# Where the short tail of a weight matrix sits, and q as columns in place of rows, in a one-token attention and GLU kernel

## The chip, the cores and the metric

The kernel runs on one core of a Trainium2 chip. The metric is the device time of one execution in microseconds. The kernel before takes 208.78 us, the median of three runs (208.6 to 209.2).

## What is computed

One token `x` of 640 numbers passes a block of attention and then a gated feed-forward block; all inputs are bfloat16.

```
h   = x + Attention(layernorm(x), k_cache, v_cache, wq, wo)
out = h + ( gelu(g) * u ) @ w_down,   g = n @ w_gate,  u = n @ w_up,  n = layernorm(h)
q = layernorm(x) @ wq           640 -> 32 heads of 128
per head: softmax(q . K / sqrt(128)) . V     K, V: 4096 x 128 per head, 32 heads
w_gate, w_up: 640 x 1728        w_down: 1728 x 640
```

K and V are 67 MB of the 84 MB that are read; the weights are the rest. Each weight is used once, so the arithmetic is matrix times vector throughout.

## The kernel before

All loads are issued by SyncE (SP) in one hand-written order: K of the first pair of heads, x, five chunks of wq, and then K and V by pairs of heads (16 pairs, 2 MB each for K and V, three buffers of each), with wo in four parts between them, then w_gate in one piece, w_up in three, and w_down in four (`wd0` to `wd3`). A load into a buffer that is used again waits for the last reader of that buffer (`load_k`, `load_v`); the loads of the feed-forward weights wait for the q stage, whose wq buffer they overwrite (L517).

**Start.** TensorE (PE) turns x into columns, takes the moments, transposes the first pair's K (`pe_transposes`), and then makes q (L318 to L343). In the kernel before q comes as rows: the normalised x (`xn_bf`) is the stationary operand, one column of it at a time, in four column groups of the array (`tile_position`), and 512 columns of wq are the moving operand. Two banks hold the rows (`qr_ps`, cleared by two matmuls with zeros, L319). VectorE and ScalarE copy the two banks to `q_row` (L585, L541), PE transposes them (L341), and VectorE picks the used columns into `q_sb` (L589). Scores of the first pair follow (`pe_scores`).

**Pairs.** A loop of five turns by three pairs: transposes of K, copies of them to SBUF by VectorE and ScalarE, P times V for the pair before, scores, softmax. All are in lock step by semaphores; wo is applied by groups of eight heads.

**End.** After the last pair: sums of the softmax (`totals`, L396), the last P times V, the projection with wo (L404), the moments of h, and then the feed-forward block. `up` (L412 to L425) makes g and then u as columns: for each of five chunks `j` of the 640 inputs, 14 matmuls of one moving column, each with 128 columns of the weight as the stationary operand. Columns 0 to 12 of the result take every 13th column of the weight (`columns(c)`, L408), so that row p of w_down's first 1664 rows falls on partition p // 13 with contiguous memory. The last column stands for the 64 columns that are left over; before, it takes the last 128 columns of the weight, 64 of which are also in the other 13 columns:

```
return slice(c, FULL * P, FULL) if c < FULL else slice(DF - P, DF)
```

The down projection (L431 to L445) goes in the order 13, 0, 1, ..., 12: five matmuls of one moving column for each. For column 13 the last 64 rows of w_down stand on partitions 64 to 127 (`wd0`, L522), and GpSimd (POOL) has cleared partitions 0 to 63 (L471), so that the columns that are taken twice count once. The other 1664 rows come in pieces of 7, 4 and 2 rows per partition (`wd1`, `wd2`, `wd3`, L524). PE waits for each piece (`landed`, L437's five-matmul groups follow).

VectorE computes `hid` from g and u (L651 to L662), adds y to h (L664), PE turns the result into rows (L447), VectorE copies it (L666), and SP writes it out.

Of the kernel before, what the change touches and what calls it, by code (L numbers as in the profile page):

```python
# [10 lines left out]
def kernel(  # L11
# [14 lines left out]
    bf16 = mybir.dt.bfloat16  # L26
# [5 lines left out]
    PE, DVE, ACT, SP, POOL = nc.tensor, nc.vector, nc.scalar, nc.sync, nc.gpsimd  # L32

    P = 128
    D = 640
    DC = D // P
    NH = 32
    DH = 128
# [11 lines left out]
    ON_ACT = (2, 5)  # L50
    DF = 1728
    NFC = 14
    FULL = NFC - 1
    LAST = DF - FULL * P
# [7 lines left out]
    pool = ctx.enter_context(tc.tile_pool(name="all", bufs=1))  # L62
    psum = ctx.enter_context(tc.tile_pool(name="ps", bufs=1, space=bass.MemoryType.PSUM))

    def sb(name, shape, dtype=f32):
        return pool.tile(shape, dtype, name=name, tag=name)
# [8 lines left out]
    wq_sb = big[:, 0 : DC * NH * DH].rearrange("p (c n) -> p c n", c=DC)  # L75
    wg_sb = big[:, 0:W_MLP].rearrange("p (c f) -> p c f", c=DC)
    wu_sb = big[:, W_MLP : 2 * W_MLP].rearrange("p (c f) -> p c f", c=DC)
    wd_sb = big[:, 2 * W_MLP :].rearrange("p (c d) -> p c d", c=NFC)

    ident = sb("ident", [P, P], bf16)  # L80
# [1 line left out]
    mean_f = sb("mean_f", [P, P])  # L82
    row_of = sb("row_of", [P, P // HG], bf16)
    col_of = sb("col_of", [P, HG], bf16)
    zero_b = sb("zero_b", [P, 4 * DH], bf16)
    x_row = sb("x_row", [DC, P], bf16)
    xs = sb("xs", [P, 2 * DC])
    xm = sb("xm", [P, 2])
    xr = sb("xr", [P, 1])
    xn_bf = sb("xn_bf", [P, DC], bf16)  # L90
    q_row = sb("q_row", [P, 2, 4 * DH], bf16)
    q_sb = sb("q_sb", [P, NH], bf16)
    q3 = sb("q3", [P, 2 * UN], bf16)
    e_t = [sb(f"ex{i}", [P, NB, 2], bf16) for i in range(UN)]
# [18 lines left out]
    hid = sb("hid", [P, NFC], bf16)  # L113
# [8 lines left out]
    tp_b = [t.bitcast(bf16) for t in tp]  # L122
    s_bank, o_bank, m_bank, a_bank = bank("s"), bank("o"), bank("m"), bank("a")
    s_ps = s_bank[:, 0 : 2 * NB].rearrange("p (j i) -> p j i", i=2)
    attn_ps = a_bank[:, 0:DC]
    qr_ps = (s_bank, o_bank)
    q_ps = tp_b[0]
    xT = m_bank.bitcast(bf16)[:, 0:DC]
    m_ps = m_bank[:, 16 : 16 + 2 * DC]
    t_ps = m_bank[:, 32 : 32 + HG]  # L130
# [1 line left out]
    g_ps, u_ps, y_ps = tp[0][:, 0:NFC], tp[1][:, 0:NFC], tp[2][:, 0:DC]  # L132
# [14 lines left out]
    S = {n: nc.alloc_semaphore(f"s_{n}") for n in names}  # L147
    done = {"pe": 0, "dve": 0, "act": 0, "pool": 0}
# [15 lines left out]
    def landed(name):  # L164

        PE.wait_ge(S[name], 16)
        PE.sem_inc(S[name], -16)  # L167
# [3 lines left out]
    def wait_pe(value):  # L171
        DVE.wait_ge(S["pe"], value)

    def dve(make, raw=True):

        if raw:
            wait(DVE, "dve", done["dve"])
        return tick("dve", make())
# [19 lines left out]
    def rstd_of(m, r):  # L198
# [6 lines left out]
        for _ in range(2):  # L205
# [3 lines left out]
            dve(lambda: DVE.tensor_tensor(y, y, w[:], ALU.mult))  # L209
        return dve(lambda: DVE.tensor_copy(r[:], y))  # L210

    PE_XT, PE_MOM, PE_QR, PE_Q = 1, 2, 12, 13
    wait_pe(PE_XT)
    dve(lambda: DVE.tensor_copy(xs[:, 0:DC], xT), False)
    DVE_XS = squares(xs)
# [3 lines left out]
    DVE_XN = dve(  # L219
        lambda: DVE.tensor_scalar(  # L220
            xn_bf[:], xs[:, 0:DC], xm[:, 0:1], xr[:], op0=ALU.subtract, op1=ALU.mult
        )
    )
    DVE_Q = DVE_XN + 2

# [20 lines left out]
    def pe_scores(q2, mark):  # L248
        for j in range(NB):
            g, b = divmod(j, GRP)  # L250
            inst = PE.matmul(
                s_ps[:, j, :],
                lhsT=ksb[g][:, b * DH : (b + 1) * DH],
                rhs=q2,
                start=True,
                stop=True,
            )
        mark("s", inst)
# [34 lines left out]
    T = {}  # L293

    def mark_at(key):
        def mark(name, inst):
            T[key, name] = tick("pe", inst)
        return mark
# [4 lines left out]
    N_DVE_T = NG - len(ON_ACT)  # L303
# [3 lines left out]
    start = mark_at("start")  # L307
# [2 lines left out]
    start("xT", PE.transpose(xT, x_row[0:DC, :], ident[0:DC, 0:DC]))  # L310
    PE.wait_ge(S["dve"], DVE_XS)
    pe_moments(xs, start)
    start("zero", PE.matmul(attn_ps, lhsT=zero_b[:, 0:P], rhs=zero_b[:, 0:DC], start=True, stop=False, skip_group_check=True))
    landed("k0")
    pe_transposes(0, 0, 0, mark_at(0))
    PE.wait_ge(S["dve"], DVE_XN)

    for b in range(2):  # L318
        PE.matmul(qr_ps[b][:], lhsT=zero_b[:, 0:P], rhs=zero_b[:], start=True, stop=False, skip_group_check=True)  # L319
    for c in range(DC):  # L320
        landed(f"wq{c}")
        for b in range(2):
            for r in range(4):
                h = 16 * b + 4 * r
                inst = PE.matmul(
                    qr_ps[b][32 * r : 32 * r + 1, :],
                    lhsT=xn_bf[:, c : c + 1],
                    rhs=wq_sb[:, c, h * DH : (h + 4) * DH],
                    start=False,
                    stop=(c == DC - 1),  # L330
                    skip_group_check=True,
                    tile_position=(0, 32 * r),
                )
    start("q rows", inst)
    PE.wait_ge(S["dve_pe"], N_DVE_T)
    PE.wait_ge(S["act_pe"], len(ON_ACT) + 1)
    PE.wait_ge(S["dve"], DVE_Q - 1)
    for b in range(2):
        for i in range(4):
            k = (4 * b + i) * P  # L340
            inst = PE.transpose(q_ps[:, k : k + P], q_row[:, b, i * DH : (i + 1) * DH], ident[:])  # L341
    start("q", inst)
    PE.wait_ge(S["dve"], DVE_Q)  # L343
    pe_scores(q_sb[:, 0:2], mark_at(0))
    PE.sem_inc(S["dve_pe"], -N_DVE_T)
    PE.sem_inc(S["act_pe"], -len(ON_ACT) - 1)
    PE.wait_ge(S["pool"], 8)

    base = done["pe"]
# [36 lines left out]


    n_turned = NP // PG - 1
    D0 = DVE_Q + 2 * n_turned
    D_SPREAD, D_ROW, D_H, D_HC, D_HID, D_Y = D0 + 4, D0 + 5, D0 + 7, D0 + 9, D0 + 9 + 14 + 10, D0 + 9 + 14 + 11  # L390

    end = mark_at("end")
# [14 lines left out]

    def columns(c):  # L408

        return slice(c, FULL * P, FULL) if c < FULL else slice(DF - P, DF)  # L410

    def up(ps, w, loads):  # L412
        for j in range(DC):
            if j in loads:
                landed(loads[j])
            for c in range(NFC):
                inst = PE.matmul(
                    ps[:, c : c + 1],
                    lhsT=w[:, j, columns(c)],
                    rhs=hc[:, j : j + 1],  # L420
                    start=(j == 0 and c == 0),
                    stop=(j == DC - 1),
                    skip_group_check=True,
                )
        return inst  # L425
# [2 lines left out]
    end("g", up(g_ps, wg_sb, {0: "wg"}))  # L428
    end("u", up(u_ps, wu_sb, {0: "wu0", 3: "wu1", 4: "wu2"}))
    PE.wait_ge(S["dve"], D_HID)  # L430
    down = {FULL: "wd0", 0: "wd1", 7: "wd2", 11: "wd3"}  # L431
    order = [FULL] + list(range(FULL))
    for i, c in enumerate(order):
        if c in down:
            landed(down[c])
        for m in range(DC):
            inst = PE.matmul(  # L437
                y_ps[:, m : m + 1],
                lhsT=wd_sb[:, c, m * P : (m + 1) * P],
                rhs=hid[:, c : c + 1],  # L440
                start=(i == 0 and m == 0),
                stop=(i == NFC - 1),
                skip_group_check=True,
            )
# [22 lines left out]

    for _ in range(2):
        spare(POOL).then_inc(S["wo"], 1)
    POOL.wait_ge(S["pe"], T["start", "q"])  # L470
    POOL.memset(wd_sb[0 : P - LAST, FULL, :], 0.0).then_inc(S["pool"], 1)  # L471
    POOL_COPIED = 9
    for g in range(NP // PG - 1):
        POOL.wait_ge(S["wo_in"], 16)
        POOL.sem_inc(S["wo_in"], -16)  # L475
# [7 lines left out]
    def load(name, dst, src):  # L483
        SP.dma_start(dst, src).then_inc(S[name], 16)
# [34 lines left out]
    wu_rows = B_w_up.rearrange("(c p) f -> p c f", p=P)  # L519
    for i, (a, b) in enumerate(((0, 3), (3, 4), (4, 5))):  # L520
        load(f"wu{i}", wu_sb[:, a:b, :], wu_rows[:, a:b, :])
    load("wd0", wd_sb[P - LAST :, FULL, :], B_w_down[FULL * P : DF, :])  # L522
    wd_rows = B_w_down[0 : FULL * P, :].rearrange("(p c) d -> p c d", c=FULL)
    WD = ((0, 7), (7, 11), (11, 13))  # L524
    for i, (a, b) in enumerate(WD):
        load(f"wd{i + 1}", wd_sb[:, a:b, :], wd_rows[:, a:b, :])

# [8 lines left out]
    for n in range(NP):  # L536
        for g in ON_ACT:
            act_copy(n, g)
        if n == 0:
            ACT.wait_ge(S["pe"], PE_QR)  # L540
            ACT.copy(q_row[:, 1, :], qr_ps[1][:]).then_inc(S["act_pe"], 1)  # L541
        ACT.wait_ge(S["pe"], pe_at(n, "s"))
        for i in range(2):
            r = slice(i * HP, (i + 1) * HP)
            inst = ACT.activation(
                e_t[n % UN][r, :, i],
                s_ps[r, :, i],
                AF.Exp,
                scale=SCALE,
                accum_out=rs_all[r, 2 * n + i : 2 * n + i + 1],  # L550
            )
            inst.then_inc(S["act"] if i == 0 else S["act_pe"], 1)
# [25 lines left out]
    def event(inst=None):  # L578
        if inst is None:
# [1 line left out]
        inst.then_inc(S["dve_pe"], 1)  # L581

    dve_copies(0)
    wait_pe(PE_QR)
    dve(lambda: DVE.tensor_copy(q_row[:, 0, :], qr_ps[0][:]), False)  # L585
    wait_pe(PE_Q)
    rows = q_ps.rearrange("p (b i r c) -> p b i r c", b=2, i=4, r=4)[:, :, :, :, 0]
    assert dve(
        lambda: DVE.tensor_copy(  # L589
            q_sb[:].rearrange("p (b r i) -> p b i r", b=2, r=4), rows  # L590
        ),
        False,
    ) == DVE_Q

    def group_of(turn):

# [2 lines left out]
    for turn in range(TURNS):  # L599
# [11 lines left out]
        if turn == 0:  # L611
            wait(DVE, "dve", DVE_Q)
        event(DVE.tensor_copy(q3[:], q_sb[:, 2 * first : 2 * (first + UN)]))
        for i in range(UN):
            n = first + i
# [12 lines left out]
        else:  # L628
            event()

    assert done["dve"] == D0
    wait_pe(T["end", "totals"])
    dve(lambda: DVE.reciprocal(rinv[:], t_ps), False)
    dve(lambda: DVE.tensor_tensor(o_col[:, 0 : HG - 2], o_raw[:, NH - HG : NH - 2], rinv[:, 0 : HG - 2], op=ALU.mult))
    wait_pe(T["end", "pv"])
# [72 lines left out]
```

## Time and profile before

| | |
|---|---|
| runs | 208.6, 209.2, 208.78 us |
| the profiled execution | 208.6 us, of which the span (first to last instruction) is 206.6 us, so 2.0 us lie around it |
| PE busy | 169.8 us (82%) |
| PE weight loads (PEld) busy | 164.3 us (79%) |
| VectorE, ScalarE, GpSimd busy | 81.0, 48.4, 19.8 us |
| bytes moved by DMA | 84.39 MB, 408 GB/s over the span |
| mean granted TensorE clock | 0.715 |

The span is read in three parts: the start up to the first scores at 24.4 us, the pairs up to some 183 us, and the end. Times in the text are microseconds from the start of the span. The form "128\*128 128x1" of a matmul is rows by columns of the stationary operand, and then the output's partitions by elements. The end of a matmul is modelled in the profile, so that the steps between the starts of matmuls are the better measure of their pace.

### The profile page before, as it was taken

Reading aid. Unit: us, or ns where it says so; the run is one execution under the profiler, and the core shown is the slowest. Engines: PE = TensorE matmul, PEld = TensorE weight load, DVE = VectorE, ACT = ScalarE, POOL = GpSimd, SP = SyncE. Lnnn points to the kernel's source line nnn. Section 1 sums busy time; section 2 is a strip of 40 time slices with the busy share of each in tenths; the row PEclk is TensorE's granted clock in tenths of the full one; section 3 lists DMA queues with packets and bytes.
Section 4 is the critical chain, followed back from the end, with each engine's and each line's share of the span. In section 5 each row is a group of like instructions: output and inputs, shape, how many; then the busy total and the mean of one; then the engine's idle time right before and its main releaser. Section 6 shows DMA issues by size and latency. Waiting matters only on the chain. (4 is left out here: it accounts for less than half of the span.)

```text
span 206.6 us, 7735 instructions
## 1 busy us (share of the span) xinstructions
PE 169.8 (82%) x3596; PEld 164.3 (79%) x3597; DVE 81.0 (39%) x199; ACT 48.4 (23%) x99; POOL 19.8 (10%) x21
## 2 busy tenths in 40 slices
PE   0295697995999999889899489999789799983893
PEld 0281497995999999788899489899789799973892
DVE  2182243432535355244435245252517162514230
ACT  0050131311313323132214113131313131310000
POOL 8200100000000006200003500000800000000000
PEclk9999558585666696759696757575757878755555
DMA  6999999999999999999999999999999999999990
GB/s 206 408 428 436 441 415 431 414 431 422 422 425 431 431 417 442 419 423 431 431 419 428 444 419 438 415 431 429 419 444 419 438 422 428 428 406 413 406 355 30
DMA packets 7791, 84.39 MB, mean 408 GB/s; under 512 B 804, under 2 KB 868, under 8 KB 2404
## 3 DMA queue, kind: packets, MB, share of 16 engines
q1 hardware_dynamic: 7780, 84.24, 97.0%
q8 instruction: 8, 0.13, 0.3%
q14 instruction: 3, 0.02, 0.0%
HBM read 84.23 MB, written 0.00 MB: 408 GB/s over the span
## 5 line engine op out<-in xcount | busy, mean ns | idle before, releaser
L562 DVE COPY ksb_67<-tp_117 128x1024 bf16<-128x1024 bf16 x16 | 11.1, 691 | 36.4 <-PE tp_117 L242 36.4
L477 POOL COPY wo<-wo_in 128x5120 bf16<-128x5120 bf16 x3 | 13.3, 4450 | 110.6 <-POOLq L475 56.0
L532 ACT COPY ksb_69<-tp_119 128x1024 bf16<-128x1024 bf16 x16 | 16.2, 1012 | 32.0 <-PE tp_119 L242 32.0
L532 ACT COPY ksb_72<-tp_118 128x1024 bf16<-128x1024 bf16 x16 | 16.2, 1012 | 18.0 <-PE tp_118 L242 17.9
L562 DVE COPY ksb_70<-tp_120 128x1024 bf16<-128x1024 bf16 x16 | 11.1, 691 | 14.8 <-PE tp_120 L242 14.8
L562 DVE COPY ksb_73<-tp_119 128x1024 bf16<-128x1024 bf16 x16 | 11.1, 692 | 6.1 <-PE tp_119 L242 5.9
L262 PE MATMUL o<-ex_94,vt_66 128*128 128x2 bf16 x320 | 8.9, 164 | 5.1 <-PEq L167 4.1
L262 PEld LDWEIGHTS o<-ex_94,vt_66 128*128 128x128 bf16 x320 | 8.7, 98 | 5.6 <-issue 4.4
L562 DVE COPY ksb_68<-tp_118 128x1024 bf16<-128x1024 bf16 x16 | 11.0, 690 | 2.0 <-PE tp_118 L242 1.9
L242 PE MATMUL tp_117<-ident,kt_63 128*128 128x128 bf16 x80 | 9.1, 283 | 3.3 <-PEq L167 3.2
L562 DVE COPY ksb_71<-tp_117 128x1024 bf16<-128x1024 bf16 x16 | 11.0, 688 | 1.6 <-PE tp_117 L242 1.6
L242 PE MATMUL tp_117<-ident,kt_61 128*128 128x128 bf16 x96 | 10.9, 283 | 0.9 <-PEq L167 0.5
L242 PE MATMUL tp_117<-ident,kt_62 128*128 128x128 bf16 x80 | 9.5, 290 | 2.4 <-PEq L167 2.4
L624 DVE COPY o_raw<-o 128x2 f32<-128x2 f32 x15 | 2.4, 159 | 21.8 <-PE o L262 21.8
L242 PE MATMUL tp_118<-ident,kt_61 128*128 128x128 bf16 x96 | 10.9, 282 | 0.0
L562 DVE COPY ksb_74<-tp_120 128x1024 bf16<-128x1024 bf16 x16 | 10.9, 680 | 0.0
L262 PE MATMUL o<-ex_92,vt_64 128*128 128x2 bf16 x384 | 10.6, 163 | 0.0
L262 PEld LDWEIGHTS o<-ex_92,vt_64 128*128 128x128 bf16 x384 | 10.4, 97 | 0.0
L242 PE MATMUL tp_119<-ident,kt_61 128*128 128x128 bf16 x96 | 10.3, 271 | 0.0
L242 PEld LDWEIGHTS tp_117<-ident,kt_63 128*128 128x128 bf16 x80 | 7.3, 131 | 3.5 <-issue 3.5
L242 PE MATMUL tp_120<-ident,kt_61 128*128 128x128 bf16 x96 | 10.0, 266 | 0.0
L242 PEld LDWEIGHTS tp_117<-ident,kt_61 128*128 128x128 bf16 x96 | 8.7, 131 | 1.3 <-DVE ksb_67 L562 0.7
(161 smaller groups left out, 320.3 us busy)
## 6 DMA issues: line engine op xcount, KB each, us to landing
kt_61<-in_A_k_cache_dram SPq DMA_DIRECT2D x6, 2048.0 KB, 25.3
vt_64<-in_A_v_cache_dram SPq DMA_DIRECT2D x6, 2048.0 KB, 27.2
kt_62<-in_A_k_cache_dram SPq DMA_DIRECT2D x5, 2048.0 KB, 24.4
kt_63<-in_A_k_cache_dram SPq DMA_DIRECT2D x5, 2048.0 KB, 26.1
vt_65<-in_A_v_cache_dram SPq DMA_DIRECT2D x5, 2048.0 KB, 28.4
vt_66<-in_A_v_cache_dram SPq DMA_DIRECT2D x5, 2048.0 KB, 30.3
big<-in_A_wq_dram SPq DMA_DIRECT2D x5, 1024.0 KB, 13.0
wo_in<-in_A_wo_dram SPq DMA_DIRECT2D x4, 1280.0 KB, 26.5
```

The lines of the kernel that those rows point to most:

```text
L242: inst = PE.transpose(tp_b[g % NBANK][:, b * DH : (b + 1) * DH], kt[slot][:, g * GRP + b, :], ident[:])
L262: inst = PE.matmul(o_bank[:, 2 * region : 2 * region + 2], lhsT=vt[slot][:, j, :], rhs=e_t[slot][:, j, :], start=(j == 0), stop=(j == NB - 1),
L477: POOL.tensor_copy(wo_t[:], wo_in[:]).then_inc(S["wo"], 1)
L532: ACT.copy(ksb[g][:], tp_b[g % NBANK][:]).then_inc(S["act_pe"], 1)
L562: DVE.tensor_copy(ksb[g][:], tp_b[g % NBANK][:]).then_inc(S["dve_pe"], 1)
L624: event(DVE.tensor_copy(o_raw[:, 2 * n - 2 : 2 * n], o_bank[:, 2 * i : 2 * i + 2]))
```

## The change

Three things are changed together.

1. q is made as columns: 160 matmuls of one moving column (`xn_bf`), each with 128 contiguous columns of wq as the stationary operand, straight into `s_bank[:, 0:32]`; one VectorE copy brings it to `q_sb`. The zero matmuls, `q_row`, its two copies and the eight transposes go.
2. The last 64 columns of w_gate and w_up are taken as 64 columns, so that the matmul for result column 13 writes 64 partitions; the last 64 rows of w_down stand on partitions 0 to 63, and their five matmuls have 64 rows. The clearing on GpSimd goes; VectorE clears partitions 64 to 127 of column 13 of g and u in PSUM (two memsets, after the wait for `totals`).
3. w_down's other rows come in pieces of 8, 4 and 1 rows per partition.

```diff
-    for b in range(2):
-        PE.matmul(qr_ps[b][:], lhsT=zero_b[:, 0:P], rhs=zero_b[:], start=True, stop=False, skip_group_check=True)
     for c in range(DC):
         landed(f"wq{c}")
-        for b in range(2):
-            for r in range(4):
-                h = 16 * b + 4 * r
-                inst = PE.matmul(
-                    qr_ps[b][32 * r : 32 * r + 1, :],
-                    lhsT=xn_bf[:, c : c + 1],
-                    rhs=wq_sb[:, c, h * DH : (h + 4) * DH],
-                    ...
-                    tile_position=(0, 32 * r),
-                )
-    start("q rows", inst)
-    ...
-            inst = PE.transpose(q_ps[:, k : k + P], q_row[:, b, i * DH : (i + 1) * DH], ident[:])
+        for h in range(NH):
+            inst = PE.matmul(
+                q_ps[:, h : h + 1],
+                lhsT=wq_sb[:, c, h * DH : (h + 1) * DH],
+                rhs=xn_bf[:, c : c + 1],
+                start=(c == 0 and h == 0),
+                ...
     start("q", inst)
...
-        return slice(c, FULL * P, FULL) if c < FULL else slice(DF - P, DF)
+        return slice(c, FULL * P, FULL) if c < FULL else slice(FULL * P, DF)
...
                 inst = PE.matmul(
-                    ps[:, c : c + 1],
+                    ps[0 : P if c < FULL else LAST, c : c + 1],
                     lhsT=w[:, j, columns(c)],
...
-    down = {FULL: "wd0", 0: "wd1", 7: "wd2", 11: "wd3"}
+    down = {FULL: "wd0", 0: "wd1", 8: "wd2", 12: "wd3"}
...
+        r = slice(0, P if c < FULL else LAST)
...
-                lhsT=wd_sb[:, c, m * P : (m + 1) * P],
-                rhs=hid[:, c : c + 1],
+                lhsT=wd_sb[r, c, m * P : (m + 1) * P],
+                rhs=hid[r, c : c + 1],
...
-    POOL.wait_ge(S["pe"], T["start", "q"])
-    POOL.memset(wd_sb[0 : P - LAST, FULL, :], 0.0).then_inc(S["pool"], 1)
...
-    load("wd0", wd_sb[P - LAST :, FULL, :], B_w_down[FULL * P : DF, :])
+    load("wd0", wd_sb[0:LAST, FULL, :], B_w_down[FULL * P : DF, :])
...
-    WD = ((0, 7), (7, 11), (11, 13))
+    WD = ((0, 8), (8, 12), (12, 13))
...
-        if n == 0:
-            ACT.wait_ge(S["pe"], PE_QR)
-            ACT.copy(q_row[:, 1, :], qr_ps[1][:]).then_inc(S["act_pe"], 1)
...
-    wait_pe(PE_QR)
-    dve(lambda: DVE.tensor_copy(q_row[:, 0, :], qr_ps[0][:]), False)
     wait_pe(PE_Q)
-    rows = q_ps.rearrange("p (b i r c) -> p b i r c", b=2, i=4, r=4)[:, :, :, :, 0]
-    ...
+    assert dve(lambda: DVE.tensor_copy(q_sb[:], q_ps), False) == DVE_Q
...
     wait_pe(T["end", "totals"])
+    dve(lambda: DVE.memset(g_ps[LAST:, FULL:], 0.0), False)
+    dve(lambda: DVE.memset(u_ps[LAST:, FULL:], 0.0), False)
```

More of the change, by code (lines that the diff above doesn't have):

```diff
@@ L84 @@
     col_of = sb("col_of", [P, HG], bf16)
-    zero_b = sb("zero_b", [P, 4 * DH], bf16)
+    zero_b = sb("zero_b", [P, P], bf16)
     x_row = sb("x_row", [DC, P], bf16)
@@ L90 @@
     xn_bf = sb("xn_bf", [P, DC], bf16)
-    q_row = sb("q_row", [P, 2, 4 * DH], bf16)
     q_sb = sb("q_sb", [P, NH], bf16)
@@ L125 @@
     attn_ps = a_bank[:, 0:DC]
-    qr_ps = (s_bank, o_bank)
-    q_ps = tp_b[0]
+    q_ps = s_bank[:, 0:NH]
     xT = m_bank.bitcast(bf16)[:, 0:DC]
@@ L210, in rstd_of @@
         return dve(lambda: DVE.tensor_copy(r[:], y))
-    PE_XT, PE_MOM, PE_QR, PE_Q = 1, 2, 12, 13
+    PE_XT, PE_MOM, PE_Q = 1, 2, 12
     wait_pe(PE_XT)
@@ L223 @@
     )
-    DVE_Q = DVE_XN + 2
+    DVE_Q = DVE_XN + 1
     def pe_transposes(slot, count_dve, count_act, mark):
@@ L312 @@
     pe_moments(xs, start)
-    start("zero", PE.matmul(attn_ps, lhsT=zero_b[:, 0:P], rhs=zero_b[:, 0:DC], start=True, stop=False, skip_group_check=True))
+    start("zero", PE.matmul(attn_ps, lhsT=zero_b[:], rhs=zero_b[:, 0:DC], start=True, stop=False, skip_group_check=True))
     landed("k0")
@@ L316 @@
     PE.wait_ge(S["dve"], DVE_XN)
-    for b in range(2):
-        PE.matmul(qr_ps[b][:], lhsT=zero_b[:, 0:P], rhs=zero_b[:], start=True, stop=False, skip_group_check=True)
     for c in range(DC):
         landed(f"wq{c}")
-        for b in range(2):
-            for r in range(4):
-                h = 16 * b + 4 * r
-                inst = PE.matmul(
-                    qr_ps[b][32 * r : 32 * r + 1, :],
-                    lhsT=xn_bf[:, c : c + 1],
-                    rhs=wq_sb[:, c, h * DH : (h + 4) * DH],
-                    start=False,
-                    stop=(c == DC - 1),
-                    skip_group_check=True,
-                    tile_position=(0, 32 * r),
-                )
-    start("q rows", inst)
[L335 to L340, printed above, removed]
-            inst = PE.transpose(q_ps[:, k : k + P], q_row[:, b, i * DH : (i + 1) * DH], ident[:])
+        for h in range(NH):
[4 more added lines that the diff above has]
+                start=(c == 0 and h == 0),
+                stop=(c == DC - 1),
+                skip_group_check=True,
+            )
     start("q", inst)
     PE.wait_ge(S["dve"], DVE_Q)
+    PE.wait_ge(S["dve_pe"], N_DVE_T)
+    PE.wait_ge(S["act_pe"], len(ON_ACT))
     pe_scores(q_sb[:, 0:2], mark_at(0))
     PE.sem_inc(S["dve_pe"], -N_DVE_T)
-    PE.sem_inc(S["act_pe"], -len(ON_ACT) - 1)
+    PE.sem_inc(S["act_pe"], -len(ON_ACT))
     PE.wait_ge(S["pool"], 8)
@@ L388 @@
     n_turned = NP // PG - 1
-    D0 = DVE_Q + 2 * n_turned
+    D0 = DVE_Q + 2 * n_turned + 2
     D_SPREAD, D_ROW, D_H, D_HC, D_HID, D_Y = D0 + 4, D0 + 5, D0 + 7, D0 + 9, D0 + 9 + 14 + 10, D0 + 9 + 14 + 11
@@ L469 @@
         spare(POOL).then_inc(S["wo"], 1)
-    POOL.wait_ge(S["pe"], T["start", "q"])
-    POOL.memset(wd_sb[0 : P - LAST, FULL, :], 0.0).then_inc(S["pool"], 1)
-    POOL_COPIED = 9
+    POOL_COPIED = 8
     for g in range(NP // PG - 1):
@@ L583 @@
     dve_copies(0)
-    wait_pe(PE_QR)
-    dve(lambda: DVE.tensor_copy(q_row[:, 0, :], qr_ps[0][:]), False)
     wait_pe(PE_Q)
-    rows = q_ps.rearrange("p (b i r c) -> p b i r c", b=2, i=4, r=4)[:, :, :, :, 0]
[L588 to L593, printed above, removed]
+    assert dve(lambda: DVE.tensor_copy(q_sb[:], q_ps), False) == DVE_Q
     def group_of(turn):
@@ L629 @@
             event()
-    assert done["dve"] == D0
+    assert done["dve"] == D0 - 2
     wait_pe(T["end", "totals"])
+    dve(lambda: DVE.memset(g_ps[LAST:, FULL:], 0.0), False)
+    dve(lambda: DVE.memset(u_ps[LAST:, FULL:], 0.0), False)
     dve(lambda: DVE.reciprocal(rinv[:], t_ps), False)
```

## The prediction, made before the changed kernel ran

> **What bounds the kernel now.** I read the slices of the span first, then the timeline of the end, then stretches of it, then the DMA issues.
>
> ```profile
> PEclk9999558585666696759696757575757878755555
> DMA  6999999999999999999999999999999999999990
> ```
>
> The DMA engines are full from the second slice to the last but one, so 84 MB set the length up to some 201 us; what is saved on PE before that is hidden, and only the end can move the time. The granted clock is 0.5 in the last five slices. The timeline of the end, PE and one VectorE row:
>
> ```profile
> 191.84 4.20 PE L417 MATMUL tp_117<-hc,big 128*128 128x1 bf16 x70 [2.84 <-PEq L167]
> 195.90 4.21 PE L417 MATMUL tp_118<-hc,big 128*128 128x1 bf16 x70
> 200.14 0.17 DVE L662 TENSOR_TENSOR hid<-g_sb,tp_118 128x14 bf16<-128x14 f32 x1 [1.78 <-PE tp_118 L417]
> 200.46 1.39 PE L437 MATMUL tp_119<-hid,big 128*128 128x1 bf16 x40 [0.35 <-PEq L167]
> 202.33 1.18 PE L437 MATMUL tp_119<-hid,big 128*128 128x1 bf16 x30 [0.48 <-PEq L167]
> 203.54 0.16 DVE L664 TENSOR_TENSOR y_bf<-hs,tp_119 128x5 bf16<-128x5 f32 x1 [3.23 <-PE tp_119 L437]
> ```
>
> g waits 2.84 us for w_gate to land. From then on PE runs without a pause through g and u to 200.1, while the DMA still works. The 40 matmuls of wd0 and wd1 are done before wd2 is there (idle 0.48), so wd2 and wd3 end last. The issues and their landings (last column, us from issue):
>
> ```profile
> big<-in_B_w_down_dram SPq DMA_DIRECT2D x1, 1120.0 KB, 15.4
> big<-in_B_w_down_dram SPq DMA_DIRECT2D x1, 640.0 KB, 15.9
> big<-in_B_w_down_dram SPq DMA_DIRECT2D x1, 320.0 KB, 15.6
> ```
>
> Issued at 185.3, 186.3 and 187.4, they land at 200.65, 202.2 and 203.0. After the last landing come ten matmuls, then y, the transpose, the copy and the output, none of which the change touches. The important point is how little PE is ahead. In the single records the last matmul of u starts at 199.94, the first weight load of the down projection at 200.43 (0.49 later, through `hid`), its matmul 0.03 after, and down matmuls step by 26.7 ns. With all data present, 70 of them would bring the last start to 199.94 + 0.49 + 0.03 + 69 x 0.0267 = 202.30; it is at 203.34. So u may end about **1.04 us** later before it costs anything.
>
> **The change, part by part.**
>
> *q as columns.* Contiguous 128-column weights with a narrow moving operand cost 26.7 ns each (64 score matmuls in 1.74 us from 24.36). 32 of them per wq chunk are 0.85 us. The last chunk is taken up at 21.08 in the trace, so q would be in PSUM at about 22.1 and in `q_sb` at 22.4 (the copy took 0.23), against scores at 24.36 now: some 1.9 us earlier. Worth nothing: the second pair's K lands at 25.9 (issued 4.57, 21.3 to landing), and PE waits for that instead. If the q stage came out longer, it would still cost nothing: when `load_k(4)` is issued at 32.19, 19.9 MB are issued and about 12.7 MB moved (29.7 us at 427 GB/s), so 17 us of work are queued. Removed copies, transposes and the GpSimd memset (0.62 us, off every path) give nothing for the same reason.
>
> *Two VectorE memsets in PSUM.* The nearest rows are 0.06 (one column) and 0.17 (128x128). At most 0.4 us for both; behind them stand the reciprocal and a product (0.4 us), and then VectorE idles 1.29 us for P times V (L636). Hidden; and behind that, g waits 2.84 us for w_gate anyway.
>
> *Pieces 8, 4, 1.* Each of 16 engines moves 8 rows of a piece. Single packets took 338 ns for 8,960 bytes, 196 for 5,120, 102 for 2,560, 55 for 1,280 and 385 for 10,240: 338 + 196 + 102 = 385 + 196 + 55, so the last landing stays at 203.0. wd2 lands 8 x (102 - 55) = 0.38 us later, at 202.6; its 20 matmuls and the five of wd3 then run through: 202.6 + 0.13 to the first matmul + 24 x 0.0267 = 203.37 for the last start, against 203.34. Nothing gained or lost. SP issues as many loads of as many rows as before.
>
> *64 columns, 64 rows.* Here I expect the time to go. PE now alternates between two shapes: in each `j`, 13 matmuls of form 128\*128, one of 128\*64, and back; ten times out, nine times back inside g and u, and from 64 rows to 128 once more in the down projection. The trace has one place where the form changes with nothing to wait for, before the q rows. PEld, then PE:
>
> ```profile
> 15.77 0.10 PEld L319 LDWEIGHTS o<-zero_b 128*128 128x128 bf16 x1
> 16.29 0.09 PEld L325 LDWEIGHTS s<-big,xn_bf 128*1 128x1 bf16 x4 [0.42 <-issue]
> 16.31 0.09 PEld L325 LDWEIGHTS o<-big,xn_bf 128*1 128x1 bf16 x4
> 15.98 0.38 PE L319 MATMUL o<-zero_b 128*128 128x512 bf16 x1
> 16.30 0.39 PE L325 MATMUL s<-big,xn_bf 128*1 128x512 bf16 x4
> 16.51 0.39 PE L325 MATMUL o<-big,xn_bf 128*1 128x512 bf16 x4
> ```
>
> Inside a form, weights are loaded ahead: at 16.31 for a matmul at 16.51. Across the change they aren't: the load at 16.29 comes after 0.42 us of idleness, though K, wq and `xn_bf` were long there. Matmuls of 512 elements step by 0.215 us (16.30, 16.51), the step across the change is 0.315. So a change of form cost **0.10 us** at full clock, plus a weight load that nothing hides.
>
> [...]
>
> At the clock of 0.5 the price is not shown: 0.10 if it doesn't scale, 0.20 if all of it does (nearly the whole 0.198 us of one L417 matmul). I take 0.15, in the middle, since neither row is nearer. Now one pair of changes. Without it, from the 13th matmul of a `j` over the 14th to the next `j`, single records step by 60 and 28 ns (193.364, 193.424, 193.452): 0.088 us; the strided loads make the 60, the contiguous one the 28. With it: twice 0.15, plus one strided load of 0.06 and one 64-column load, taken at 0.04 between those two. That is 0.40, so 0.31 us more per pair. Nine pairs and one change out (0.15 + 0.04 - 0.06 = 0.13): 9 x 0.31 + 0.13 = **2.9 us** on the end of u. In the down projection one more change (0.15) comes behind the five matmuls of wd0. Sum 3.05 - 1.04 = **2.0 us** at the end.
>
> With 0.10: a pair costs 0.21, in all 1.97 + 0.10, net 1.0 us. With 0.20: 0.41, in all 3.87 + 0.20, net 3.0 us. Below nothing is excluded: even a free change would leave the landing of wd2 and wd3 last. GELU's chain between g and u (2.3 us from 196.08) moves with g by half the delay and stays ahead of u.
>
> [...]
>
> **Rivals.**
>
> *No cost (the other side).* The change of form at 16.3 went from 128 columns to one column in four groups. If 64 columns in the first group don't drain the array, or for under 0.05 us, u ends less than 1.04 us later and the landings decide as before: no change, 208.6 to 208.9. For it: a single row of another form. Against it: that row's idleness has no other cause in the trace. The point from which it decides is 0.09 us more per pair.
>
> *An instruction fetch on the wrong DMA engine.* Eight instruction packets of 16 KB (the second queue of the page) took about 1.06 us each, and each left one engine some 1.5 us behind: the spread between the first and last engine's landing of a load rose from 0.7 us at 25.9 to 1.7 at 31.7, after the packet at 26.6. The ten or so fetches before the end hit different engines. q as columns writes out 110 more matmuls, 220 more instructions on some 2,230, which is 0.8 of a packet. On an engine that is already late it would move the last landing by up to 1.5 us: 210.2 without the drain. With the drain of my forecast it is covered, as PE would need wd3 only at about 205. The packets so far speak for a fresh engine.
>
> *Gain.* Two fewer rows behind the last landing can't pay, since wd2 lands later. The only gain on paper is the last engine's lag, 2.1 us at the end against 1.9 before: 0.2 us, under what can be measured.
>
> **How the numbers follow.** The profiled execution took 208.6 us, 0.18 below the median of the runs, 208.78. Forecast: 208.6 + 2.0 + 0.18 = 210.8, as a median; its own range 209.7 to 211.9 from the two ends of the drain. Chances: drain that decides 0.72, no cost 0.17, a fetch or another cost of that size 0.06, a gain of which I see no mechanism 0.05. About 0.3%, or 0.6 us, is what a measurement of this kernel can tell from no change. The small end of the drain still lies above that. Faster 0.05, same 0.16, slower 0.79. The range reaches from the no-cost case to the upper end: 208.7 to 211.9.
>
> **What would show it.** Right: L417 split in runs of 13 with a gap of some 0.2 us on either side of the 128\*64 row, g and u together about 11 us in place of 8.3, no idleness before wd2 and wd3, y at about 205.5. The scores start near 22.5 with no effect on later landings. Wrong: L417 still in 4.2 us each, and idleness ahead of wd2; or a last landing clearly after 203.0.

## The result, and the profile after

The changed kernel takes 209.62 us (median of six runs, 209.52 to 210.39) against 208.62 us of the kernel before (six runs beside it): a ratio of 1.0051, 95% interval 1.0032 to 1.007. It is 1.0 us slower, where the forecast was 2.0 us. The profiled execution took 209.52 us with a span of 207.7 us.

The end of the changed kernel, from its timeline (start, length, engine and line, what):

```profile
191.88 5.13 PE L403 MATMUL tp_116<-hc,big 128*128 128x1 bf16 x70 [1.05 <-DVE rs_v L200]
196.95 5.15 PE L403 MATMUL tp_117<-hc,big 128*128 128x1 bf16 x70
202.14 0.17 DVE L639 TENSOR_TENSOR hid<-g_sb,tp_117 128x14 bf16<-128x14 f32 x1 [2.81 <-PE tp_117 L403]
202.46 2.12 PE L424 MATMUL tp_118<-hid,big 64*128 64x1 bf16 x70 [0.35 <-PEq L165]
204.61 0.16 DVE L641 TENSOR_TENSOR y_bf<-hs,tp_118 128x5 bf16<-128x5 f32 x1 [2.30 <-PE tp_118 L424]
```

g and u take 5.1 us each in place of 4.2, `hid` comes 2.0 us later, and the down projection is one run of 70 matmuls without a pause that the timeline shows: in this view PE ends last, and no longer the landings. So far this is the forecast's mechanism. But the DMA has changed as well. The row of the instruction queue, before and then after:

```profile
q8 instruction: 8, 0.13, 0.3%
q8 instruction: 9, 0.15, 0.3%
```

Stretches of the last microseconds (stretch, its length, busy time of PE, weight loads, VectorE, ScalarE and GpSimd, granted clock, DMA share, GB/s). The first row is the kernel before, the others are the changed one:

```profile
202.50:202.75 0.25, 0.25 (x15) 0.25 (x13) 0.00 (x0) 0.00 (x0) 0.00 (x0) 0.50 0.00 0
202.00:202.50 0.50, 0.15 (x3) 0.09 (x4) 0.17 (x1) 0.00 (x0) 0.00 (x0) 0.50 0.26 100
202.50:203.00 0.50, 0.50 (x18) 0.49 (x19) 0.00 (x0) 0.00 (x0) 0.00 (x0) 0.50 0.09 36
203.00:203.50 0.50, 0.50 (x25) 0.50 (x22) 0.00 (x0) 0.00 (x0) 0.00 (x0) 0.50 0.05 18
```

There are nine instruction packets where there were eight, and from 202.5 us on, where before nothing was left to move, the DMA share is 0.09 and then 0.05. One engine of sixteen that still works while the others are done would give 1/16, or 0.06, by estimate. In the single records of the landings 15 engines are through with `wd3` at 203.08, the last at 204.04; before, the last two came at 202.80 and 202.97. The issues say the same (`wd1`, `wd2`, `wd3`, us to landing 16.9, 17.3 and 16.6, against 15.4, 15.9 and 15.6):

```profile
big<-in_B_w_down_dram SPq DMA_DIRECT2D x1, 1280.0 KB, 16.9
big<-in_B_w_down_dram SPq DMA_DIRECT2D x1, 640.0 KB, 17.3
big<-in_B_w_down_dram SPq DMA_DIRECT2D x1, 160.0 KB, 16.6
```

PE takes up `wd3` at 204.30, a quarter of a microsecond after it landed. For `wd2` the two are nearly level: it landed at 203.64, and its first matmul starts at 203.77. That is 0.13 us after the landing, as it was before (202.19 and 202.33), and 53 ns after the matmul ahead of it, where the others step by 27. So PE stood 0.03 us for the data after all. Two things ended 1.0 us later, side by side, and the profile alone doesn't tell which of them the microsecond is due to.

### The profile page after: what moved, and what is told of

It is laid out like the page before. It is cut to its first block, busy times and chain, and to the rows that moved or that the text cites. A ratio compares the mean times of both kernels' runs of the same rounds, so it can differ in the third digit from the quotient of the medians.

```text
span 207.7 us, 7955 instructions
## 1 busy us (share of the span) xinstructions
PE 173.3 (83%) x3707; PEld 170.2 (82%) x3707; DVE 79.9 (38%) x200; ACT 47.8 (23%) x98; POOL 19.2 (9%) x20
## 5 line engine op out<-in xcount | busy, mean ns | idle before, releaser
L240 PE MATMUL tp_116<-ident,kt_62 128*128 128x128 bf16 x80 | 9.6, 293 | 4.1 <-PEq L165 4.1
L240 PE MATMUL tp_116<-ident,kt_61 128*128 128x128 bf16 x96 | 11.6, 295 | 1.5 <-DVE ksb_67 L544 0.7
L240 PE MATMUL tp_117<-ident,kt_61 128*128 128x128 bf16 x96 | 11.3, 289 | 1.8 <-issue 1.8
L240 PEld LDWEIGHTS tp_116<-ident,kt_62 128*128 128x128 bf16 x80 | 7.7, 135 | 4.4 <-issue 4.4
L240 PEld LDWEIGHTS tp_117<-ident,kt_61 128*128 128x128 bf16 x96 | 9.5, 137 | 2.2 <-issue 2.1
L240 PE MATMUL tp_116<-ident,kt_63 128*128 128x128 bf16 x80 | 9.1, 282 | 2.3 <-PEq L165 2.3
L240 PEld LDWEIGHTS tp_116<-ident,kt_61 128*128 128x128 bf16 x96 | 9.2, 136 | 1.8 <-DVE ksb_67 L544 0.9
L240 PE MATMUL tp_118<-ident,kt_61 128*128 128x128 bf16 x96 | 10.4, 272 | 0.0
```

The lines of the kernel that those rows point to most:

```text
L240: inst = PE.transpose(tp_b[g % NBANK][:, b * DH : (b + 1) * DH], kt[slot][:, g * GRP + b, :], ident[:])
```

## The experiments

Theory D: the drain, which here is a name for the pause that PE makes at each change of form between 128\*128 and 128\*64 (in the changed kernel steps of 130 and 144 ns where the kernel before has 60 and 28; what the array does in it no record shows). Theory F: q as columns writes out 220 more PE instructions, a ninth instruction packet comes ahead of the last landing, and it falls on a DMA engine that one of the first eight had already put behind (no record names the engine of a packet; the landings have to tell). Each ratio is to the kernel before on the same chip, with its 95% interval; the runs come from several chips, so times of different experiments are better compared by their ratios. What the kernel before took on the same chip is 208.7 to 209.0 us.

**Part 2 alone: 64 columns and 64 rows, q as rows.** All of part 2 is in, with the load of `wd0`, GpSimd's clearing and the two memsets as in the changed kernel; the diff shows the matmuls.

```diff
 (kernel before)
-        return slice(c, FULL * P, FULL) if c < FULL else slice(DF - P, DF)
+        return slice(c, FULL * P, FULL) if c < FULL else slice(FULL * P, DF)
...
-                    ps[:, c : c + 1],
+                    ps[0 : P if c < FULL else LAST, c : c + 1],
...
-                lhsT=wd_sb[:, c, m * P : (m + 1) * P],
-                rhs=hid[:, c : c + 1],
+                lhsT=wd_sb[r, c, m * P : (m + 1) * P],
+                rhs=hid[r, c : c + 1],
...
```

> The kernel before with part 2 of the change alone: 64 columns of w_gate and w_up, 64 rows of w_down on partitions 0 to 63, q still as rows, pieces 7, 4, 2. Theory D (the drain at each change of form moves the end of u): u ends 1.95 us later as in the changed kernel, less some 1.0 us of slack, so about +1.0 us, 209.6, and PE never idle in the down projection. Theory F (the instructions that q as columns adds move an instruction fetch onto a DMA engine that is already late, and the last landing goes from 203.0 to 204.0): no added PE instructions, so the last landing stays at 203.0 and the time at 208.6.

Measured: 209.58 us against 208.74, ratio 1.0032 (1.0022 to 1.0043). Its PE rows:

```profile
191.94 10.23 PE L417 MATMUL tp<-hc,big 128*128 128x1 bf16 x140 [2.98 <-DVE rs_y L209]
202.52 2.09 PE L438 MATMUL tp<-hid,big 64*128 64x1 bf16 x70 [0.35 <-PEq L167]
```

g and u as long as in the changed kernel, no pause before any piece. Eight packets came ahead of the last landing, which is at 203.33, some 0.9 us before PE takes up `wd3`. The changes of form alone cost 0.8 us by the medians, 0.5 to 0.9 by the interval.

**Part 1 alone: q as columns.** The edit is all of part 1 of the change, and nothing else of it.

> The kernel before with part 1 alone: q as columns, all else as before. Theory D: 140 matmuls of g and u in 8.2 us as before, end unchanged, 208.6. Theory F: nine instruction packets in place of eight, the last landing at about 204.0 in place of 203.0, PE idle before wd3, and the end about 1.0 us later, 209.6. If both hold, the two parts cost 1 us each and not 2 us together, since each covers the other.

Measured: 209.9 us, ratio 1.0052 (1.0032 to 1.0072). Its PE rows:

```profile
192.08 8.26 PE L403 MATMUL tp<-hc,big 128*128 128x1 bf16 x140 [2.97 <-DVE rs_y L207]
200.69 0.27 PE L423 MATMUL tp<-hid,big 128*128 128x1 bf16 x5 [0.35 <-PEq L165]
202.08 1.07 PE L423 MATMUL tp<-hid,big 128*128 128x1 bf16 x35 [1.11 <-PEq L165]
203.62 1.20 PE L423 MATMUL tp<-hid,big 128*128 128x1 bf16 x30 [0.48 <-PEq L165]
```

g and u are as fast as before, and PE stands before `wd1` for 1.11 us: the first matmul of `wd1` starts 1.28 us after the one ahead of it, where it was 0.21 before. Nine packets, the ninth at 199.29. On 15 engines `wd3` is there at 202.93, on the last at 204.28. So the part that the prediction priced at nothing costs about a microsecond by itself.

**The changed kernel with the 64-column matmuls gathered.**

```diff
 (changed kernel)
-            for c in range(NFC):
+            for c in range(FULL):
                 inst = PE.matmul(
-                    ps[0 : P if c < FULL else LAST, c : c + 1],
+                    ps[:, c : c + 1],
                     ...
+        for j in range(DC):
+            inst = PE.matmul(
+                ps[0:LAST, FULL : FULL + 1],
+                lhsT=w[:, j, columns(FULL)],
+                rhs=hc[:, j : j + 1],
+                start=False,
+                ...
```

> The changed kernel, with the five 64-column matmuls of g (and of u) put together behind the 65 others, so that the form changes twice per product and not ten times. Theory D: about 0.3 us of changes for g and 0.3 for u, under the 1.0 us of slack, so the drain costs nothing and the time goes back to 208.6. Theory F: the late landing at 204.0 is then bare, PE waits for wd3, and the time stays near 209.6.

Measured: 209.71 us, ratio 1.0039 (1.0026 to 1.0053).

```profile
201.03 0.27 PE L433 MATMUL tp<-hid,big 64*128 64x1 bf16 x5 [0.35 <-PEq L165]
202.58 1.21 PE L433 MATMUL tp<-hid,big 128*128 128x1 bf16 x40 [1.27 <-PEq L165]
204.16 0.81 PE L433 MATMUL tp<-hid,big 128*128 128x1 bf16 x25 [0.38 <-PEq L165]
```

The down projection can begin at 201.03 in place of 202.46, and gains nothing from it: it waits 1.27 us for `wd1`. With most of the changes of form gone, the late engine (204.40, the others by 203.35) shows alone.

**110 more matmuls in the kernel before**, which add zeros, at a place where the start is covered.

```diff
 (kernel before)
+    for _ in range(110):
+        PE.matmul(attn_ps, lhsT=zero_b[:, 0:P], rhs=zero_b[:, 0:DC], start=False, stop=False, skip_group_check=True)
     landed("k0")
```

> The kernel before with 110 more matmuls (220 PE instructions) that add zeros to the projection's bank, right after the matmul that clears it at 9.7 us; q as rows, forms and pieces as before. Theory D: the delay of 3 us at the start is hidden by the DMA queue, 208.6. Theory F: the same number of added instructions as in the changed kernel moves the fetches in the same way, nine packets, the last landing near 204.0, 209.6. If the fetch falls on a fresh engine, 208.6 too.

Measured: 209.92 us, ratio 1.0045 (1.0029 to 1.0061). Nine packets, the last at 199.52, 15 engines through by 203.17 and the last at 204.17. Nothing of q, of a form or of a piece differs from before; the added instructions alone bring the microsecond.

**30 in place of 110** (the same edit with `range(30)`).

> The kernel before with 30 more matmuls at 9.7 us in place of the 110 of the run before. Theory F (a ninth instruction packet ahead of the last landing falls on a DMA engine that already had one): 60 instructions move each fetch by 60 instructions, the eighth to about 197 us and the ninth to about 203, when the loads are over; last landing near 203.0, time 208.7. Theory S (each added instruction costs, or the start itself): 30/110 of the 1.0 us, 209.0.

Measured: 208.84 us against 208.76, ratio 0.9998 (0.9986 to 1.0011). The eighth packet came at 196.64, the ninth at 207.92 when all was over; the last landing is at 203.24. It isn't the added work as such; what matters is whether the ninth packet comes ahead of the last landing.

**64 columns gathered, with q as rows.** Part 2 alone with the edit of the third experiment.

> The kernel before (q as rows, pieces 7, 4, 2) with 64 columns and 64 rows, the five 64-column matmuls of each product behind the 65 others. Theory D: two changes of form per product, g and u together some 8.9 us, under the slack, and eight packets: 208.7, about 0.9 us less than with the 64-column matmul inside each chunk. If the 64 columns or rows cost by themselves (and not by the alternation), the time stays near 209.6.

Measured: 208.57 us, ratio 0.9992 (0.9977 to 1.0008). Eight packets, last landing 202.95:

```profile
195.87 0.42 PE L426 MATMUL tp<-hc,big 128*64 128x1 bf16 x5
196.23 4.09 PE L417 MATMUL tp<-hc,big 128*128 128x1 bf16 x65
200.25 0.42 PE L426 MATMUL tp<-hc,big 128*64 128x1 bf16 x5
201.03 2.46 PE L447 MATMUL tp<-hid,big 64*128 64x1 bf16 x70 [0.35 <-PEq L167]
```

The five 64-column matmuls of a product now step by 53 to 54 ns behind the first two, and u's last matmul starts at 200.48, 0.54 us later than before; that is inside the 1.04 us that PE has to spare. So the alternation makes the microsecond, and 64 columns or 64 rows put together don't show in the time. The third experiment has the same order of matmuls and the ninth packet; here, with neither cause left, the time is that of before.

**q as columns for half of the heads.** It leaves out q of heads 16 to 31, for which q of heads 0 to 15 is used again.

```diff
 (part 1 alone)
-        for h in range(NH):
+        for h in range(NH // 2):
...
-    assert dve(lambda: DVE.tensor_copy(q_sb[:], q_ps), False) == DVE_Q
+    dve(lambda: DVE.tensor_copy(q_sb[:, 0 : NH // 2], q_ps[:, 0 : NH // 2]), False)
+    assert dve(lambda: DVE.tensor_copy(q_sb[:, NH // 2 :], q_ps[:, 0 : NH // 2]), False) == DVE_Q
```

> Part 1 alone, but q of heads 0 to 15 only, which heads 16 to 31 use again: it leaves out 80 of the 160 matmuls of q. 160 instructions fewer than with all heads, 60 more than in the kernel before. Theory F: the ninth packet comes after the last landing, 208.7, though q is made as columns. If q as columns costs in another way (its chain at the start, its place in the bank), the time is between 208.7 and 209.8, about 209.2 or more.

Measured: 208.68 us, ratio 0.9997 (0.9988 to 1.0006). Eighth packet at 196.66, ninth at 207.71, last landing 203.02. Making q as columns costs nothing that shows when the ninth packet comes after the loads.

**Part 3 alone: pieces of 8, 4 and 1.**

> The kernel before with part 3 alone: w_down in pieces of 8, 4 and 1 rows per partition. Both theories: last landing near 203.0, wd2 0.38 us later, no wait between wd2's and wd3's matmuls, 208.7 within 0.2. If the small packets cost more than the single ones show, up to 0.4 us more.

Measured: 208.54 us, ratio 0.9987 (0.9973 to 1.0001). `wd2` landed at 202.60 and `wd3` at 203.01, as worked out from the packets (202.6, 203.0); the last matmul started at 203.38 (203.37). No difference that can be told.

**Twice the changes of form.** Part 2 alone, with the 64-column matmul of each chunk in two of 32 columns, one after the sixth matmul and one at the end.

```diff
 (part 2 alone)
             for c in range(NFC):
+                if c == FULL // 2 or c == FULL:
+                    half = LAST // 2
+                    lo = 0 if c < FULL else half
+                    inst = PE.matmul(
+                        ps[lo : lo + half, FULL : FULL + 1],
+                        lhsT=w[:, j, FULL * P + lo : FULL * P + lo + half],
+                        ...
```

> Part 2 alone with twice the changes of form: the 64-column matmul of each chunk cut into two of 32 columns, one after the sixth matmul and one at the end, 20 pairs of changes in g and u in place of 10. Theory D, with 0.187 us for each further pair as the changed kernel's records show: u ends another 1.9 us later, none of it covered any more, so 1.9 us above part 2 alone, 211.4. If a drain is shorter for fewer columns, or the second one partly free, less than 1 us above.

Measured: 211.29 us, ratio 1.0113 (1.0089 to 1.0137). The first chunk of g shows the alternation row by row:

```profile
192.33 0.18 PE L420 MATMUL tp<-hc,big 128*32 128x1 bf16 x1
192.44 0.57 PE L429 MATMUL tp<-hc,big 128*128 128x1 bf16 x7
192.95 0.19 PE L420 MATMUL tp<-hc,big 128*32 128x1 bf16 x1
193.06 0.53 PE L429 MATMUL tp<-hc,big 128*128 128x1 bf16 x6
```

The down projection starts at 204.23 in place of 202.52 with part 2 alone: 1.71 us for ten more pairs of changes, 0.17 each with the extra matmul in between. The time is longer by as much: the ratio rises by 0.008, which is 1.7 us. Once the slack is used up, each pair is paid in full.

**230 more matmuls in the kernel before** (460 instructions).

> The kernel before with 230 more matmuls at 9.7 us, 460 instructions: a ninth and a tenth packet ahead of the last landing. Theory F with packets that go round eight DMA engines: the ninth and the tenth fall on two engines that each had one before; both are late, the last landing at about 204.2 as with 110 matmuls, 209.8. If later packets pile up on one engine: 205.5 and 211. If the tenth is after the loads: 209.8 as well, with one late engine.

Measured: 210.06 us, ratio 1.0042 (1.0024 to 1.006). Ten packets ahead of the last landing, the ninth at 190.48 and the tenth at 200.92, and two engines late: 204.47 and 204.57, the other 14 by 203.13. The load that landed at 193.38 lies between the ninth packet and the tenth: 15 engines came within 2.08 us of the first, and one at 3.47. So a ninth packet that comes 13 us ahead of the end puts one engine behind all the others as well; in these runs it is the count that does it, and not that the packet comes shortly before the last landing. Two late engines, and not one that is late by two packets, is what theory F expected if packets go round eight engines; that they do was not shown, since the records don't name the engine.

**Parts 2 and 3, 64 columns gathered, q as rows.**

> Parts 2 and 3 with the 64-column matmuls behind the others, q as rows, eight packets: neither cost of the changed kernel is left, and GpSimd's clearing is gone. 208.5 to 208.7, the same as before within what can be measured; the only version in this series that could be below the kernel before.

Measured: 208.76 us against 208.96, ratio 0.999 (0.9979 to 1.0001): the same as before. No version of the series is faster than the kernel before by more than can be measured.

## Why the prediction was wrong

**What held.** The length is set by DMA up to 201 us (DMA share 1.03 from 191.8 to 200.0 us in the changed kernel), and only the end moves the time. q comes earlier with no effect that lasts on the loads that follow it (the one that lands at 178.47 before lands at 178.55). The memsets are hidden (0.06 us each). The pieces change nothing (208.54 us with them alone). PE had 1.04 us to spare at the end of u. Each change of form holds PE up (steps of 128 to 146 ns), and by itself (the first experiment) this gives about the time of the changed kernel. q came earlier by less than forecast: the scores start at 23.63 and not near 22.5, since the last chunk of wq is taken up at 22.35 in place of 21.08. One of the prediction's own signs of being wrong also came true: a last landing clearly after 203.0.

**The term that was mis-sized.** A pair of changes was put at 0.40 us: twice 0.15 for the drain and 0.10 for two weight loads that nothing hides. In the single records of the changed kernel the matmul before the change starts at 193.628, the 64-column load at 193.756, its matmul at 193.758, the next strided load at 193.898 and its matmul at 193.902. The steps are 130 and 144 ns, 0.275 us for the pair, and the matmul starts 2 and 4 ns after its load: the drain's 0.128 and 0.140 is all there is, and the 0.10 for the loads doesn't exist as a term of its own. This is the step that failed. (The row of the trace before had shown this too, with a load at 16.293 and a matmul at 16.295; I had read the 0.10 of the drain from it and not the 2 ns; by single records its step is 0.310, so 0.095 beyond the 0.215.)

At the granted clock of 0.50 the drain, 0.128 and 0.140 us, is between my ends of 0.10 and 0.20. A pair costs 0.187 more than without it, not 0.31: nine pairs and the last change out make 1.75 us in place of 2.9. With a start of g 0.04 later and some 0.16 us of slower steps in the rest (the matmul behind each change back came 80 to 89 ns before the next, and not 60), u's last matmul came 1.95 us later, at 201.89. The change behind `wd0` cost 0.07 (a step of 94 ns in place of 27), not 0.15. 1.95 + 0.07 - 1.04 is 0.98; the last matmul started 1.07 us later, 204.41 against 203.34. That the time lies at the lower end of the sum, 1.0 us, is partly luck: that end stood for a drain of 0.10 with the loads on top. (The two ends give 209.8 and 211.8 as times; the range of 209.7 to 211.9 in the prediction is a little wider than its sum.)

The forecast's 0.04 us for a 64-column load was an estimate between the steps of 60 and 28 ns of the two other loads. Behind a change such a load doesn't show as time of its own, with the matmul 2 ns after its load (193.756 and 193.758); where the 64-column matmuls follow each other in the gathered kernels, they step by 53 to 54 ns.

**The rival that was misjudged.** What no step of mine allowed was that the fetch rival is true at the same time. I gave it 0.06, since the packets so far seemed to have hit different engines. The landings of the kernel before agree with that (the page counts eight packets, not ten or so): in the loads behind the first six packets 1, 2, 4, 5, 6 and 7 engines land more than 0.9 us after the first, and behind the eighth none lands more than 2.14 us after it. Behind the ninth, which 0.8 of a packet made likely, the last landing of the changed kernel came 3.05 us after the first, with 2.08 for the next one. That the ninth met an engine that was already late is read from these landings. The reason "worth nothing" for q as columns looked at PE and at the queued loads alone, and put the added instructions at no time. Six kernels side by side, all with the old forms of matmul, so that no drain is in them (the landings are of `wd3`, by single records):

| kernel | packets ahead of the last landing | last landing, us | the engines before it, us | time |
|---|---|---|---|---|
| before | 8 | 202.97 | 202.80 | 208.62 |
| 30 more matmuls | 8 | 203.24 | 202.99 | 208.84 |
| half of q as columns | 8 | 203.02 | 202.93 | 208.68 |
| 110 more matmuls | 9 | 204.17 | 203.17 | 209.92 |
| q as columns | 9 | 204.28 | 202.93 | 209.9 |
| 230 more matmuls | 10 | 204.57, 204.47 | 203.13 | 210.06 |

In the changed kernel the two causes cover each other almost exactly: the last matmul starts 1.07 us late, and by the 0.03 us for which PE stood at `wd2`, it would have started at 204.41 without the drain and at 204.38 without the late engine. That is why undoing one cause alone gives next to nothing back (the first experiment undoes the ninth packet, the second and the third the alternation), while undoing both does. The forecast's size was wrong mainly by the 0.10 per pair; had the size been right, the reason "q as columns: worth nothing" would still have been wrong, and the time would have hidden it.

## What to carry to other kernels

Where two forms of matmul alternate, count the changes and not the matmuls: here each pair cost 0.17 to 0.20 us, and putting the odd ones together brought the delay under the slack that PE had. Written-out instructions had a DMA price here that no PE row shows (packets of 16 KB and some 1.07 us each, and 1.0 us of time for the ninth); compare the number of instruction packets and the last engine's landing before and after, also where the added work itself is hidden. When a part is said to cost nothing, run it alone: a cost that another one covers shows in neither the time nor the chain that ended last.

## What the hardware showed that was not expected

The eight instruction packets of 16 KB in the kernel before took 1.02 to 1.10 us each, 1.07 on the mean. Before the first packet all engines land a load within 0.70 us (at 25.87, kernel before); in the next one (at 31.73) 15 do, and one comes at 1.67, and it isn't made up later: this kernel's loads are still spread over 1.9 us at 186 us. After six packets, in the load that ends at 186.47, eight engines land within 0.45 us of the first and eight 0.78 to 1.89 us after it; after eight the last load is spread over 2.12 us. It was the ninth, and not the first eight, that moved the last landing, by 1.0 to 1.35 us against the other engines. Ten packets made two such engines. A count changed by 60 instructions was harmless (208.84 us), one changed by 220 was not (209.92 us). And in the down projection the change from 64 rows back to 128 took 94 ns, less than the 128 to 146 between 128 and 64 columns in g and u, at the same clock of 0.5.
